# A check at the seam of two stages: most of it is emitted into the attention, and its end is cut to one maximum

## The chip, the cores and the metric

The kernel runs on one core of one Trainium2 chip. Five engines work side by side, each with its own stream of instructions in program order: PE (TensorE, matrix products), DVE (VectorE), ACT (ScalarE), POOL (GpSimd) and SP (SyncE, which here issues most DMAs). The metric is the device time of one execution in microseconds, median of several runs.

## The reference

An attention in which each query keeps only its 32 largest scores feeds a mixture of experts with a greedy, capacity-bound assignment of tokens.

```python
scores = scale * np.matmul(q, k.transpose(0, 1, 3, 2))       # batch 8, heads 8, seq 576, head_dim 64
kth = np.partition(scores, -32, axis=-1)[..., -32:-31]
scores = np.where(scores >= kth, scores, -1000000000.0)
attn = np.exp(scores - np.max(scores, axis=-1, keepdims=True))
attn = attn / (np.sum(attn, axis=-1, keepdims=True) + 1e-09)
x = heads_side_by_side(np.matmul(attn, v))                   # 4608 tokens x 512
logits = x @ w_gate                                          # 8 experts
order = np.argsort(-logits.flatten())
for idx in order:                                            # each token to one expert, 576 per expert
    tok, e = (int(idx) // E, int(idx) % E)
    if assigned[tok] >= 0 or counts[e] >= cap: continue
    assigned[tok] = e; counts[e] += 1
for e in range(E):
    mask = assigned == e
    out[mask] = np.maximum(x[mask] @ w1[e], 0.0) @ w2[e]
```

## The kernel before

The kernel has three parts, one after the other: `attention`, `redo` and `moe`.

`attention` works on 32 pairs of heads (8 batches, 4 pairs each). A pair has 9 tiles of 128 queries against 576 keys. For each tile PE makes the scores (L218) in one of three PSUM buffers; DVE finds maxima of six chunks (L221, called `c0` to `c5` in the plan) and ranks them (L224 to L228, `k0` to `k4`) to the 24th largest; ACT takes a sign against it and counts into one column of `acc` (L233); DVE writes a filling (L239), PE shifts the kept scores away and back (L236), DVE finds the next eight maxima, of which the 32nd largest is one (L240); ACT makes the mask (L243). Later, in `soft`, PE computes transposed scores with the mask (L281 to L287), ACT the exponential (L291), POOL splits it into two halves of float16 by a copy and a subtraction (L294, L297), and PE multiplies with V (L365). `tail` does the same for the last 64 keys (L319 to L327). DVE and ACT normalise (L345 to L347). POOL copies each pair's thresholds into `cuts` (L309). After the third pair of a batch, and again after the fourth, `logits` adds its part of x @ w_gate to the tile `L` (last additions L421 and L422), and `store` writes x to DRAM.

The order in which the instructions are emitted comes from a list planner on the host (`Plan`): every step has an engine, an assumed duration, predecessors and a due time; on each engine, among the steps that can start within a small window, the one with the smallest due time is emitted next. A due time is the tile's nominal start (4.9146 per tile) plus an offset from the table `O`, for instance 138.764 for `c0`, 131.547 for `c2` and 127.672 for `c5`. The chip's engines then run their streams in that order.

After the planned part, `verdict` (L424 and following) tests whether the fast way of finding thresholds was right everywhere: for all 288 tiles the count in `acc` must be a whole number in bounds and the threshold positive, and every logit must be finite. It sums the good ones per pair and per group of logits over partitions by a product with ones on PE (L447), and writes one flag per pair and the number of flags set (L448 to L454). Then `redo` loads that number into a register of every engine (L485) and branches (L486); in its body, which isn't entered for these inputs, flagged pairs are computed again in a slow and exact way.

`moe` then picks the experts in turn from `L` by bisection, gathers the tokens, and runs the two matrix products. Its first steps on DVE are at L621 and following.

Of the kernel before, what the change touches and what calls it, by code (L numbers as in the profile page):

```python
# [7 lines left out]
F32 = mybir.dt.float32  # L8
# [88 lines left out]

VS=64.0
QS=256.0
def attention(tc, q,k,v,w_gate,x_out,L,flags, pairs):  # L100
    NCH=6
    nc=tc.nc
    CW=576//NCH; NCAND=8*NCH
    with ExitStack() as ctx:
# [284 lines left out]
        def logits(P,part):  # L389
# [28 lines left out]
            else:  # L418
# [2 lines left out]
                piece(0,[lambda c=c: P["x"][0][:,c,384:512] for c in range(4)],512,dots,lambda lg: V.tensor_tensor(main.rearrange("p c e -> p (c e)"),lg[:,:32],main.rearrange("p c e -> p (c e)"),op=ALU.add))  # L421
                piece(1,*corner(1),lambda lg: V.tensor_tensor(last,lg[o:o+64,:8],last,op=ALU.add))  # L422
            P["fin"]=at(t0,lambda: None,fin); P["lgdone"]=fin[-1]
        def verdict():  # L424

            n9=len(pairs)*9; npr=len(pairs)
            c=cp.tile([128,n9],F32,name="vc"); r=cp.tile([128,n9],F32,name="vr"); ok=cp.tile([128,n9],F32,name="vok")
            V.tensor_scalar(c,acc,-0.5,-256.0,op0=ALU.mult,op1=ALU.add)
            V.tensor_scalar(r,c,12582912.0,None,op0=ALU.add)
            V.tensor_scalar(r,r,-12582912.0,None,op0=ALU.add)  # L430
            V.tensor_tensor(ok,r,c,op=ALU.is_equal)
            V.scalar_tensor_tensor(ok,c,8.0,ok,op0=ALU.is_le,op1=ALU.mult)
            V.scalar_tensor_tensor(ok,c,0.0,ok,op0=ALU.is_ge,op1=ALU.mult)
            V.scalar_tensor_tensor(ok,cuts,0.0,ok,op0=ALU.is_gt,op1=ALU.mult)
            good=cp.tile([128,npr+4],F32,name="good")
            V.tensor_reduce(good[:,:npr],ok.rearrange("p (n i) -> p n i",i=9),axis=AX.X,op=ALU.add)
            whole=[]
            for k,(u0,u1) in enumerate(((0,28),(32,35),(28,32),(35,36))):
                Lf=L[:,u0:u1,:].rearrange("p t e -> p (t e)"); w=8*(u1-u0); fin=cp.tile([128,w],F32,name=f"fin{k}")
                V.tensor_tensor(fin,Lf,Lf,op=ALU.subtract)  # L440
                V.tensor_scalar(fin,fin,0.0,None,op0=ALU.is_equal)
                V.tensor_reduce(good[:,npr+k:npr+k+1],fin,axis=AX.X,op=ALU.add); whole.append(128.0*w)
            ones=cp.tile([128,1],F32,name="ones1"); V.memset(ones,1.0)
            want=cp.tile([1,npr+4],F32,name="want"); V.memset(want[:,:npr],1152.0)
            for k,x_ in enumerate(whole): V.memset(want[:,npr+k:npr+k+1],x_)
            pt=ps_t.tile([128,512],F32,tag="pt",name="ptv")
            T.matmul(pt[:1,:npr+4],ones,good,start=True,stop=True)  # L447
            bad=cp.tile([1,npr+4],F32,name="bad"); V.tensor_tensor(bad,want,pt[:1,:npr+4],op=ALU.subtract)  # L448
            nf=cp.tile([1,1],F32,name="nf"); V.tensor_reduce(nf,bad[:,npr:],axis=AX.X,op=ALU.add)
            V.tensor_scalar(bad[:,:npr],bad[:,:npr],nf,None,op0=ALU.add)  # L450
            fl=cp.tile([1,npr],F32,name="flf"); V.tensor_scalar(fl,bad[:,:npr],0.0,None,op0=ALU.not_equal)
            V.tensor_reduce(nf,fl,axis=AX.X,op=ALU.add)
            V.tensor_copy(flags[:,npr:npr+1],nf)
            V.tensor_copy(flags[:,0:npr],fl)  # L454

        Ps={}; batch={}
        for n in range(len(pairs)):
            prep(n); P=Ps[n]; b=P["b"]
            P.update(st=None,tr={},mx={},rel={},q2={},ev={},teh={},soft={},x=[None,None])
            first=P["hp"]==0  # L460
            def begin(P=P,n=n,first=first):
                P["st"]=wk.tile([128,9,33],F32,tag="st",name="st",bufs=3)
                P["x"]=(wk.tile([128,4,512],F32,tag="xb",name="xb",bufs=2),wk.tile([128,4,64],F32,tag="xr",name="xr",bufs=2)) if first else Ps[n-1]["x"]
            pre=[Ps[n-3]["done"]] if n>2 else []
            if n: pre.append(Ps[n-1]["begin"])
            if first and b>1: pre.append(batch[b-2])
            P["begin"]=at(n*9*PER+O["S"]-0.01,begin,pre)
            for i in range(9): tile_ops(P,i)
            for i in range(9): soft(P,i)
            clear(P)  # L470
            tail(P)
            values(P)
            if P["hp"]==2: logits(P,0)
            if P["hp"]==3:
                P["done"]=at(P["done"]["t"]+.001,lambda: None,[P["done"],Ps[n-1]["fin"]])
                logits(P,1); P["done"]=P["fin"]; batch[b]=at((n*9+8)*PER+O["lg"]+O["lgd"]*5,lambda P=P: store(P),[P["fin"]],e="D",d=2.0,late=4.0)
        loom.run()
        verdict()


def redo(tc,q,k,v,w_gate,x,L,flags):

    nc=tc.nc
    V,G,A,T=nc.vector,nc.gpsimd,nc.scalar,nc.tensor
    any_=nc.values_load(flags[0:1,32:33],min_val=0,max_val=32)  # L485
    with tc.If(any_>0):  # L486
        with ExitStack() as ctx:
            cp=ctx.enter_context(tc.tile_pool(name="rc",bufs=1))
            wk=ctx.enter_context(tc.tile_pool(name="rw",bufs=2))
            ps=ctx.enter_context(tc.tile_pool(name="rps",bufs=2,space=PSUM))  # L490
            ident=cp.tile([128,128],F32,name="identr"); make_identity(nc,ident)
            wg=cp.tile([128,4,8],F32,name="wgf"); nc.sync.dma_start(out=wg,in_=w_gate.rearrange("(c p) e -> p c e",p=128))
            qv,kv,vv=(t.rearrange("b (g t) s d -> b g t s d",t=2) for t in (q,k,v))
# [102 lines left out]
def moe(tc, K, L, x, w1, w2, out):  # L596
# [4 lines left out]
    with ExitStack() as ctx:  # L601
# [3 lines left out]
        wp=ctx.enter_context(tc.tile_pool(name="wp",bufs=2))  # L605
        ps=ctx.enter_context(tc.tile_pool(name="ps",bufs=1,space=PSUM))
        V,G,A,P,S=nc.vector,nc.gpsimd,nc.scalar,nc.tensor,nc.sync
        O=dict(RT=341.23, TE=-289.219, TN=-172.671, WT=261.813, XT=32.643, RD=-297.654, GL=2.6, W_V=0.1, W_A=0.395, W_G=2.142, W_P=0.0, W_D=9.225, WD0=678.788, WD1=322.634, RA=-247.153, WT0=9.992, TE0=-55.559, XT0=-502.675)
        GL,RT,TE,TN,WT,XT,RD,RA,WT0,TE0,XT0=(O[k] for k in ('GL','RT','TE','TN','WT','XT','RD','RA','WT0','TE0','XT0')); WD=(O['WD0'],O['WD1'])
        WIN={e:O['W_'+e] for e in 'VAGPD'}  # L610
        HOW0='vvvvvvvv'; HOW='vvvvvvvv'; GP=3; AHV=1; JO=1; PB=3; SPN=512
        plan=Plan(dict(ph=4,po=2,wr=4,W=2,xT=2,hh=1,xg=4,ob=3),WIN);
# [319 lines left out]
        c=Chain(-RT)  # L932
        for p in range(E):
            c.pre=[X[p-1]["next"]]+([X[p-2]["idx"]] if p>1 else []) if p else []
            c.t=p*47.0-RT
            route(p,c)
            enlist(p,Chain(c.t+(TE if p else TE0),X[p]["sel"],X[p-1]["idx"] if p else None))
            weigh(p,p*47.0-(WT if p else WT0))
            bring(p,p*47.0-XT if p else XT0)
            ffn(p,p*47.0)  # L940
# [3 lines left out]
def attention_then_moe(tc, q, k, v, w_gate, w1, w2, out):  # L944
    with ExitStack() as ctx:
        dp = ctx.enter_context(tc.tile_pool(name="dp", bufs=1, space=DRAM))
        lp = ctx.enter_context(tc.tile_pool(name="lp", bufs=1))
        x = dp.tile([4608, 512], F32, name="x")
        L = lp.tile([128, 36, 8], F32, name="L")
        pairs = [(b, hp) for b in range(8) for hp in range(4)]  # L950
        flags = lp.tile([1, 40], I32, name="flags")
        K = moe_consts(tc, lp)
        attention(tc, q, k, v, w_gate, x, L, flags, pairs)
        redo(tc, q, k, v, w_gate, x, L, flags)
        moe(tc, K, L, x, w1, w2, out)


# [25 lines left out]
```

## Time and profile before

| | us |
|---|---|
| median of 3 runs | 1455.42 (1453.14 to 1456.38) |
| the profiled execution | 1456.97 |
| its span, from the first instruction to the last | 1455.2 |
| DVE busy in the span | 1208.0 (83%) |
| PE busy | 1291.6 (89%) |
| POOL busy | 878.1 (60%) |
| ACT busy | 863.5 (59%) |

The profiled execution is 1.55 us above the median of the others. Times within the trace count from the span's start. A share of busy time is a mean over stages which have different limits, so it says little by itself about one place.

### The profile page before, as it was taken

What the parts mean: (1) busy time and instruction counts of PE and PEld (TensorE: products, weight loads), DVE (VectorE), ACT (ScalarE), POOL (GpSimd) and SP (SyncE); (2) the same over time, 40 slices, a digit from 0 to 9 for tenths busy, and PEclk for the clock granted to TensorE, in tenths of its full rate; (3) what the DMA queues carried; (4) which work ended last, traced back from release to release, by engine and by line L of the source; (5) the groups of instructions that cost most, each with busy time, mean ns of one, the idle gap of its engine ahead of it and who ended that gap; (6) DMA issues with size and microseconds to landing.
All of it is one profiled execution on the core that took longest, in us unless ns stands there. A gap on an engine that the chain in (4) does not pass through costs nothing. (4 is left out here: it accounts for less than half of the span.)

```text
span 1455.2 us, 41655 instructions
## 1 busy us (share of the span) xinstructions
PE 1291.6 (89%) x15019; PEld 908.3 (62%) x15020; DVE 1208.0 (83%) x6010; ACT 863.5 (59%) x1898; POOL 878.1 (60%) x1285
## 2 busy tenths in 40 slices
PE   2889999999999999999999999834989999999997
PEld 1667776776776766776676776723655655655663
DVE  5899999899999999999999999578879878878510
ACT  2677777777777777787787787603324424424421
POOL 5687888798798788789789879402123123133211
PEclk8899999999999999999999999955999999999999
DMA  5434444444345444454445442104336447448500
GB/s 123 90 84 75 113 100 86 102 87 99 94 95 106 78 111 91 85 117 90 88 113 85 87 110 43 41 6 148 132 83 200 145 83 199 145 87 279 114 33 33
DMA packets 293384, 148.47 MB, mean 102 GB/s; under 512 B 250672, under 2 KB 275248, under 8 KB 292144
## 3 DMA queue, kind: packets, MB, share of 16 engines
q1 hardware_dynamic: 287280, 126.84, 38.4%
q0 software_dynamic: 5888, 18.88, 4.4%
q8 instruction: 120, 1.97, 0.6%
q14 instruction: 96, 0.79, 0.2%
HBM read 71.34 MB, written 18.87 MB: 62 GB/s over the span
## 5 line engine op out<-in xcount | busy, mean ns | idle before, releaser
L221 DVE MAX8 cd<-s 128x8 f32<-128x96 f32 x1728 | 373.5, 252 | 35.3 <-PE s L218 30.6
L297 POOL TENSOR_TENSOR elm<-F,ehm 128x512 f16<-128x512 f32 x256 | 294.7, 1157 | 7.9
L243 ACT ACTIVATE r<-s,st 128x576 bf16<-128x576 f32 x288 | 213.2, 740 | 106.5 <-PE s L236 70.5
L233 ACT ACTIVATE w<-s,st 128x576 uint16<-128x576 f32 x288 | 213.5, 741 | 79.7 <-DVE st L229 76.8
L240 DVE MAX8 st<-s 128x8 f32<-128x584 f32 x288 | 220.8, 767 | 7.4 <-PE s L236 2.6
L218 PE MATMUL s<-K,Q 128*128 128x512 f16 (+3 forms) x1280 | 193.0, 291 | 27.8 <-DMA Q<-nq 20.2
L890 PE MATMUL ph<-xT,w1h 128*128 128x288 f16 x1024 | 196.3, 289 | 2.7 <-DMA xT<-xs 2.2
L929 POOL DMA_INDIRECT out_dram<-ob,idx x40 | 54.9, 1372 | 223.8 <-ACT ob L924 157.4
L287 PE MATMUL pt<-Q,K 66*128 66x128 f16 (+1 forms) x1280 | 179.1, 216 | 0.1
L286 PE MATMUL pt<-Q,K 128*128 128x128 f16 (+1 forms) x1280 | 178.2, 215 | 0.0
L294 POOL TENSOR_SCALAR ehm<-F 128x512 f16<-128x512 f32 x256 | 157.2, 620 | 32.3 <-ACT F L291 29.8
L218 PEld LDWEIGHTS <-Q 128*128 128x128 f16 (+1 forms) x1280 | 104.8, 103 | 108.5 <-DMA Q<-nq 19.9
L236 PE MATMUL s<-w,off 128*128 128x512 f16 x576 | 132.6, 288 | 38.6 <-DVE s L239 30.3
L850 POOL DMA_INDIRECT xg<-x,idx x40 | 51.7, 1292 | 179.0 <-DVE idx L796 107.3
L291 ACT ACTIVATE F<-pt 128x512 f32<-128x512 f32 x256 | 150.7, 597 | 14.8 <-PE pt L287 9.9
L890 PE MATMUL ph<-xT,w1l 128*128 128x288 f16 x512 | 148.1, 289 | 0.0
L365 PE MATMUL pv<-vt,E 128*64 128x65 f32 (+1 forms) x1024 | 146.8, 257 | 0.3 <-DVE L L416 0.3
L236 PE MATMUL s<-w,back 128*128 128x512 f16 x576 | 118.7, 288 | 20.6 <-DVE st L240 18.3
L899 ACT ACTIVATE hh<-ph 128x288 f16<-128x288 f32 x128 | 52.4, 410 | 130.1 <-PE ph L890 125.6
L286 PEld LDWEIGHTS <-K 128*128 128x128 f16 x1280 | 117.2, 99 | 18.4 <-issue 5.5
L365 PEld LDWEIGHTS <-ehm 128*128 128x128 f16 x2048 | 115.9, 101 | 9.8
L365 PEld LDWEIGHTS pv<-vt,E 128*64 128x64 f32 (+1 forms) x1024 | 113.2, 164 | 13.5 <-issue 3.1
(262 smaller groups left out, 3342.4 us busy)
## 6 DMA issues: line engine op xcount, KB each, us to landing
wr<-in_moe_w_dram SPq DMA_DIRECT2D x32, 1024.0 KB, 9.5
kn<-in_k_dram SPq DMA_DIRECT2D x64, 128.0 KB, 2.4
qn<-in_q_dram SPq DMA_DIRECT2D x64, 128.0 KB, 2.3
vn<-in_v_dram SPq DMA_DIRECT2D x64, 128.0 KB, 2.3
x<-xb SPq DMA_DIRECT2D x8, 1024.0 KB, 4.6
Q<-nq SPq DMA_TRANSPOSE x160, 2.5
kn<-in_k_dram SPq DMA_DIRECT2D x64, 16.0 KB, 2.2
qn<-in_q_dram SPq DMA_DIRECT2D x64, 16.0 KB, 2.1
```

Of the source, the lines that this page charges most:

```text
L218: T.matmul(s_ps[rows,a:b_],P[Q][:,qc],P[K][:,h*576+a:h*576+b_],start=(Q=="Q1"),stop=(Q=="Q2"))
L221: V.max(D["cd"][:,c*8:c*8+8],D["s"][:,576*c//NCH:576*(c+1)//NCH])
L233: A.activation(D["w"],D["s"][:,:576],AF.Sign,bias=P["st"][:,i,32:33],scale=(1+2.0**-21),accum_out=acc[:,col])
L236: T.matmul(D["s"][:,a:b_],by,w[:,a:b_],start=False,stop=True,skip_group_check=True)
L240: def next8(): V.max(P["st"][:,i,24:32],D["s"][:,:584])
L243: A.activation(r,D["s"][:,:576],AF.Relu,bias=P["st"][:,i,31:32],scale=-1.0)
L286: T.matmul(o,K2[:,kb:kb+128],Q1[:,qc],start=False,stop=False,skip_group_check=True)
L287: T.matmul(o,K3[0:66,kb:kb+128],Q2[0:66,qc],start=False,stop=(c==3 and h==sub[-1][0]),skip_group_check=True)
L294: G.tensor_scalar(D["eh"],D["E"],1.0,0.0,op0=ALU.mult,op1=ALU.add)
L297: G.tensor_tensor(el,D["E"],D["eh"],op=ALU.subtract); P["e"][i]=(D["eh"],el)
L365: for m_ in (range(N-1) if part==0 else (N-1,)): T.matmul(out,seq[m_][0],seq[m_][1],start=(m_==0),stop=(m_==N-1))
L890: P.matmul(B["ph"][:,:288],a[:,c,fs],xT[:,b+c,cs],start=(i==0),stop=(i==11))
```

## The change

The check is taken apart. `judge(n0,n1)` holds its eight steps for the thresholds of some pairs, `finite(k)` its three steps for one group of logits; each returns its steps as a list of functions. `ahead` hands the thresholds of the first 30 pairs and the logits of the first seven batches (two groups) to the planner, as DVE steps of an assumed 0.35 us that follow one another, with the last tile's nominal start as their due time and with the cuts of pairs 28 and 29, or the end of pair 27, as predecessors. `verdict` does the rest, the last two pairs and the last batch's two groups, with the three chains interleaved. After the sum on PE it takes one maximum over what is missing, and writes the minimum of it and 1 as the flag that is branched on. The sums over the flags, and the flags of the single pairs, are made inside the branch of `redo`, from the tile `bad`, which is now allocated outside. The constants `ones` and `want` are set before the planned part. A name `R1` with the value 0.0 is added to a due time in `moe`.

```diff
-def attention(tc, q,k,v,w_gate,x_out,L,flags, pairs):
+def attention(tc, q,k,v,w_gate,x_out,L,flags,bad, pairs):
...
+        npr=len(pairs); spans=((0,28),(32,35),(28,32),(35,36)); early=npr-2
+        good=cp.tile([128,npr+4],F32,name="good"); ones=cp.tile([128,1],F32,name="ones1"); V.memset(ones,1.0)
+        want=cp.tile([1,npr+4],F32,name="want"); V.memset(want[:,:npr],1152.0)
+        for s_,(u0,u1) in enumerate(spans): V.memset(want[:,npr+s_:npr+s_+1],128.0*8*(u1-u0))
+        def judge(n0,n1):
+            cs=slice(n0*9,n1*9); w=9*(n1-n0); B={}
+            def a0(): B["c"]=cp.tile([128,w],F32,name=f"vc{n0}"); V.tensor_scalar(B["c"],acc[:,cs],-0.5,-256.0,op0=ALU.mult,op1=ALU.add)
+            def a1(): B["r"]=cp.tile([128,w],F32,name=f"vr{n0}"); V.tensor_scalar(B["r"],B["c"],12582912.0,None,op0=ALU.add)
+            def a2(): V.tensor_scalar(B["r"],B["r"],-12582912.0,None,op0=ALU.add)
+            def a3(): B["ok"]=cp.tile([128,w],F32,name=f"vok{n0}"); V.tensor_tensor(B["ok"],B["r"],B["c"],op=ALU.is_equal)
+            def a4(): V.scalar_tensor_tensor(B["ok"],B["c"],8.0,B["ok"],op0=ALU.is_le,op1=ALU.mult)
+            def a5(): V.scalar_tensor_tensor(B["ok"],B["c"],0.0,B["ok"],op0=ALU.is_ge,op1=ALU.mult)
+            def a6(): V.scalar_tensor_tensor(B["ok"],cuts[:,cs],0.0,B["ok"],op0=ALU.is_gt,op1=ALU.mult)
+            def a7(): V.tensor_reduce(good[:,n0:n1],B["ok"].rearrange("p (n i) -> p n i",i=9),axis=AX.X,op=ALU.add)
+            return [a0,a1,a2,a3,a4,a5,a6,a7]
+        def finite(k):
+            u0,u1=spans[k]; w=8*(u1-u0); Lf=L[:,u0:u1,:].rearrange("p t e -> p (t e)"); B={}
+            def a0(): B["f"]=cp.tile([128,w],F32,name=f"fin{k}"); V.tensor_tensor(B["f"],Lf,Lf,op=ALU.subtract)
+            def a1(): V.tensor_scalar(B["f"],B["f"],0.0,None,op0=ALU.is_equal)
+            def a2(): V.tensor_reduce(good[:,npr+k:npr+k+1],B["f"],axis=AX.X,op=ALU.add)
+            return [a0,a1,a2]
+        def ahead():
+            t=((npr-1)*9+8)*PER
+            for fs,pre in ((judge(0,early),[Ps[early-1]["clear"],Ps[early-2]["clear"]]),(finite(0),[Ps[npr-5]["done"]]),(finite(1),[Ps[npr-5]["done"]])):
+                for f in fs: pre=[at(t,f,pre,e="V",d=.35)]
         def verdict():
...
+            j_,f2,f3=judge(early,npr),finite(2),finite(3)
+            for a in (f2[0],f3[0],j_[0],f2[1],f3[1],j_[1],f2[2],f3[2],*j_[2:]): a()
             pt=ps_t.tile([128,512],F32,tag="pt",name="ptv")
             T.matmul(pt[:1,:npr+4],ones,good,start=True,stop=True)
-            bad=cp.tile([1,npr+4],F32,name="bad"); V.tensor_tensor(bad,want,pt[:1,:npr+4],op=ALU.subtract)
-            nf=cp.tile([1,1],F32,name="nf"); V.tensor_reduce(nf,bad[:,npr:],axis=AX.X,op=ALU.add)
-            V.tensor_scalar(bad[:,:npr],bad[:,:npr],nf,None,op0=ALU.add)
-            fl=cp.tile([1,npr],F32,name="flf"); V.tensor_scalar(fl,bad[:,:npr],0.0,None,op0=ALU.not_equal)
-            V.tensor_reduce(nf,fl,axis=AX.X,op=ALU.add)
-            V.tensor_copy(flags[:,npr:npr+1],nf)
-            V.tensor_copy(flags[:,0:npr],fl)
+            V.tensor_tensor(bad,want,pt[:1,:npr+4],op=ALU.subtract)
+            m=cp.tile([1,1],F32,name="most"); V.tensor_reduce(m,bad,axis=AX.X,op=ALU.max)
+            V.tensor_scalar(flags[:,npr:npr+1],m,1.0,None,op0=ALU.min)
...
+        ahead()
         loom.run()
         verdict()
...
-    any_=nc.values_load(flags[0:1,32:33],min_val=0,max_val=32)
+    any_=nc.values_load(flags[0:1,32:33],min_val=0,max_val=1)
     with tc.If(any_>0):
...
+            nf=cp.tile([1,1],F32,name="nf"); V.tensor_reduce(nf,bad[:,32:],axis=AX.X,op=ALU.add)
+            V.tensor_scalar(bad[:,:32],bad[:,:32],nf,None,op0=ALU.add)
+            fl=cp.tile([1,32],F32,name="flf"); V.tensor_scalar(fl,bad[:,:32],0.0,None,op0=ALU.not_equal)
+            V.tensor_copy(flags[:,0:32],fl)
...
-            c.t=p*47.0-RT
+            c.t=p*47.0-RT+(R1 if p==1 else 0)
```

## Rows read from the trace of the kernel before

**Rows 1.** Stretches: us, each engine's busy time (instructions), PE's clock, DMA share, GB/s.

```profile
877.00:909.00 32.00, 29.72 (x414) 21.47 (x414) 30.05 (x172) 24.88 (x59) 29.88 (x47) 1.00 0.25 48
...
947.00:955.00 8.00, 0.28 (x2) 0.12 (x2) 6.46 (x33) 0.00 (x0) 0.00 (x0) 0.50 0.00 0
```

**Rows 2.** Timeline of DVE, last logits to first step of moe: start, length, line.

```profile
946.58 0.17 DVE L422 TENSOR_TENSOR L<-lg,L 64x8 f32<-64x8 f32 x1 [0.34 <-PE lg L410]
946.76 0.31 DVE L428 TENSOR_SCALAR vc<-acc 128x288 f32<-128x288 f32 x1
...
947.79 0.46 DVE L431 TENSOR_TENSOR vok<-vr,vc 128x288 f32<-128x288 f32 x1
...
950.20 0.38 DVE L440 TENSOR_TENSOR fin<-L 128x224 f32<-128x224 f32 x1
...
952.48 0.17 DVE L441 TENSOR_SCALAR fin<-fin 128x8 f32<-128x8 f32 x1
952.69 0.16 DVE L442 TENSOR_REDUCE good<-fin 128x1 f32<-128x8 f32 x1
...
953.32 0.18 DVE L448 TENSOR_TENSOR bad<-want,ptv 1x36 f32<-1x36 f32 x1 [0.39 <-PE ptv L447]
...
954.46 0.16 DVE L454 CAST flags<-flf 1x32 int32<-1x32 f32 x1
960.12 0.07 DVE L621 MEMSET pen<- 128x8 f32 x1 [5.50 <-SPq L486]
```

**Rows 3.** DVE's waits from 845 to 928: total us, times, longest us.

```profile
DVE cd L221 <- PE s L218: 0.8, 3, 0.3
...
DVE st L240 <- PE s L236: 0.2, 1, 0.2
```

**Rows 4.** Timeline of DVE in moe, two chains interleaved, eight starts apart.

```profile
986.97 0.23 DVE L756 TENSOR_SCALAR w8c<-rev,win 128x8 f32<-128x8 f32 x1
...
987.84 0.45 DVE L667 TENSOR_TENSOR ml<-L,pen 128x288 f32<-128x288 f32 x1
988.21 0.19 DVE L771 SCALAR_TENSOR_TENSOR qf<-qf 128x36 f32<-128x36 f32 x1
```

**Rows 5.** Timelines of POOL and DVE, what the moved steps must follow.

```profile
876.25 0.21 POOL L309 TENSOR_SCALAR cuts<-st 128x9 f32<-128x9 f32 x1
...
848.69 0.14 DVE L422 TENSOR_TENSOR L<-lg,L 64x8 f32<-64x8 f32 x1
```

**Rows 6.** Timelines of POOL and DVE at the kernel's start.

```profile
2.80 0.65 POOL L592 IOTA exf<- 32x512 f32 x1
...
2.79 0.18 DVE L576 CAST tk<-thi 128x36 f32<-128x36 int32 x1
2.88 0.61 DVE L576 CAST tk<-tlo 128x36 f32<-128x36 int32 x1
```

**Rows 7.** POOL's two lines of soft: shortest, median, longest in ns; first and last start.

```profile
L294 POOL TENSOR_SCALAR ehm<-F x256: 614/620/627, 38.4 to 936.6; 128x512 f16<-128x512 f32 x128
...
L297 POOL TENSOR_TENSOR elm<-F,ehm x256: 1149/1157/1168, 39.1 to 937.3; 128x512 f16<-128x512 f32 x128
```

**Rows 8.** Timelines of DVE, POOL, ACT and PE in the attention's drain.

```profile
929.73 0.77 DVE L240 MAX8 st<-s 128x8 f32<-128x584 f32 x1 [0.56 <-PE s L236]
...
933.75 0.60 ACT L327 ACTIVATE E<-pt 128x512 f32<-128x512 f32 x1 [0.25 <-PE pt L324]
...
935.45 0.19 PE L365 MATMUL pv<-vh,ehm 128*128 128x65 f16 x1
...
938.12 0.16 DVE L345 TENSOR_SCALAR rs<-pv 128x4 f32<-128x4 f32 x1 [6.92 <-PE pv L365]
...
916.00 0.20 POOL L265 TENSOR_SCALAR m<-st 128x3 f32<-128x3 f32 x1 [5.45 <-DVE st L224]
...
937.26 1.15 POOL L297 TENSOR_TENSOR elm<-F,ehm 128x512 f16<-128x512 f32 x1
```

**Rows 9.** Timeline of DVE, its first step of the planned part.

```profile
21.43 1.42 DVE L221 MAX8 cd<-s 128x8 f32<-128x96 f32 x8 [13.73 <-PE s L218]
```

More of the change, by code (lines that the diff above doesn't have):

```diff
@@ L423, in logits @@
             P["fin"]=at(t0,lambda: None,fin); P["lgdone"]=fin[-1]
-        def verdict():
[L426 to L445, printed above, removed]
@@ L476, in attention, with redo @@
                 logits(P,1); P["done"]=P["fin"]; batch[b]=at((n*9+8)*PER+O["lg"]+O["lgd"]*5,lambda P=P: store(P),[P["fin"]],e="D",d=2.0,late=4.0)
+        ahead()
         loom.run()
         verdict()
-def redo(tc,q,k,v,w_gate,x,L,flags):
+def redo(tc,q,k,v,w_gate,x,L,flags,bad):
     nc=tc.nc
     V,G,A,T=nc.vector,nc.gpsimd,nc.scalar,nc.tensor
-    any_=nc.values_load(flags[0:1,32:33],min_val=0,max_val=32)
+    any_=nc.values_load(flags[0:1,32:33],min_val=0,max_val=1)
     with tc.If(any_>0):
@@ L607, in moe @@
         V,G,A,P,S=nc.vector,nc.gpsimd,nc.scalar,nc.tensor,nc.sync
-        O=dict(RT=341.23, TE=-289.219, TN=-172.671, WT=261.813, XT=32.643, RD=-297.654, GL=2.6, W_V=0.1, W_A=0.395, W_G=2.142, W_P=0.0, W_D=9.225, WD0=678.788, WD1=322.634, RA=-247.153, WT0=9.992, TE0=-55.559, XT0=-502.675)
-        GL,RT,TE,TN,WT,XT,RD,RA,WT0,TE0,XT0=(O[k] for k in ('GL','RT','TE','TN','WT','XT','RD','RA','WT0','TE0','XT0')); WD=(O['WD0'],O['WD1'])
+        O=dict(RT=341.23, R1=0.0, TE=-289.219, TN=-172.671, WT=261.813, XT=32.643, RD=-297.654, GL=2.6, W_V=0.1, W_A=0.395, W_G=2.142, W_P=0.0, W_D=9.225, WD0=678.788, WD1=322.634, RA=-247.153, WT0=9.992, TE0=-55.559, XT0=-502.675)
+        R1,GL,RT,TE,TN,WT,XT,RD,RA,WT0,TE0,XT0=(O[k] for k in ('R1','GL','RT','TE','TN','WT','XT','RD','RA','WT0','TE0','XT0')); WD=(O['WD0'],O['WD1'])
         WIN={e:O['W_'+e] for e in 'VAGPD'}
@@ L951, in attention_then_moe @@
         flags = lp.tile([1, 40], I32, name="flags")
+        bad = lp.tile([1, 36], F32, name="bad")
         K = moe_consts(tc, lp)
-        attention(tc, q, k, v, w_gate, x, L, flags, pairs)
-        redo(tc, q, k, v, w_gate, x, L, flags)
+        attention(tc, q, k, v, w_gate, x, L, flags, bad, pairs)
+        redo(tc, q, k, v, w_gate, x, L, flags, bad)
         moe(tc, K, L, x, w1, w2, out)
```

## Prediction

> **What bounds the kernel now.** I read the table of stretches first. Up to 930 us the attention keeps PE, DVE and POOL busy together: of 32 us between 877 and 909, DVE works 30.05 and POOL 29.88. Between 947 and 955 only DVE works, POOL and DMA not at all, and PE sits at a granted clock of 0.50 [rows 1]. That hole is the step that the change cuts. The timeline of DVE shows what is in it: the last logits are added at 946.58 (done 946.75), then verdict() runs as one chain until the flags are written at 954.46 + 0.16 = 954.62, and DVE does nothing more until 960.12 [rows 2]. So the check costs 7.87 us with no cover, and 5.50 us follow in which all engines read the flag and jump over redo(). There is no work of verdict() in those, so I leave them as they are.
>
> Next I ask what bounds the place to which the work goes. The list of DVE's waits between 845 and 928 holds four entries, one of 0.8 us and three of 0.2 us, 1.4 us in 83 [rows 3]. DVE waits for nobody there: in that part it is the bound, or so near to it that whatever is added to its stream comes out later at its end.
>
> **What verdict() still costs.** 17 DVE instructions stay between the last logits and the flag: six for the logits of the last batch, eight on 18 columns for the last two pairs, then subtraction, maximum and minimum with the write. The trace has prices for both kinds of spacing. Small instructions that need not wait for each other start 0.11 us apart (eight starts from 986.97 to 987.84, 0.87 us) [rows 4]. One that needs its predecessor starts 0.21 us after it (952.48 to 952.69) [rows 2]. The first nine are interleaved three ways, so they take the short spacing: first start 946.76, ninth at 946.76 + 8 x 0.11 = 947.64. Five more each need the one before: 947.64 + 5 x 0.21 = 948.69, done 0.18 later at 948.87. The sum over partitions on PE: from the last reduction's end (952.69 + 0.16 = 952.85) to the subtraction's start at 953.32 are 0.47 us [rows 2], of which about 0.08 were memsets that now run at the kernel's start: 0.39, so 949.26. Maximum and minimum each 0.21 later: 949.68, done 949.82. The flag is there 954.62 - 949.82 = **4.8 us** earlier. If nothing overlaps, 13 x 0.21 replaces 8 x 0.11 + 5 x 0.21 and 4.0 are left; if the first starts ahead of the last logits, 4.9. The flags of the single pairs move into the branch, which isn't entered, and cost nothing.
>
> **What moves into the attention.** Fourteen DVE instructions: eight on 270 columns for the first 30 pairs, three on 224 and three on 24 for the early logits. Their due time in the plan is that of the last tile, (31 x 9 + 8) x 4.9146 = 1410.5. The plan takes, among what DVE can start at once, what has the smallest due time. A tile's first chunk maximum has its tile's start + 138.8, the third + 131.5, the sixth + 127.7, so from tile 259 on (in pair 28) these come after 1410.5, and the moved steps go ahead of them as soon as they are ready. Ready means: after pair 29's cuts, on POOL at 876.25, and after the logits of pair 27, whose last addition is at 848.69 [rows 5]. I therefore expect them near 849 and from 877 to 887, not in the drain. They bring no DMA.
>
> Their time on DVE: a 288-wide one-source step takes 0.31, a two-input step 0.46 [rows 2], and with an independent neighbour the next one starts 0.08 before the end (0.45 long, next start after 0.37) [rows 4]. Eight steps: 3 x 0.23 + 4 x 0.38 + 0.37 = 2.58, for 270 columns 2.4. The three on 224 columns, of which the first took 0.38 [rows 2], about 0.8, the three on 24 at 0.1 each 0.3: 3.5 us. Some fall between two steps of a rank chain that would start 0.21 apart and then fill a gap of 0.1 each, at most 1.4 for fourteen; I take half: **2.8 us** (2.1 if all do so, 4.6 if nothing overlaps).
>
> Then POOL. At the kernel's start a one-source DVE step of 36 columns begun at 2.79 takes 0.18 us. Its twin, begun at 2.88 beside POOL's iota of 2.80 to 3.45, takes 0.61 and ends at 3.49, just after POOL [rows 6]. So a one-source step between SBUF tiles is held until POOL's running instruction ends. In the attention before the change none is held and none holds: POOL's 256 copies and 256 subtractions lie within 614 to 627 and 1149 to 1168 ns [rows 7], since DVE there reads scores from PSUM or runs at the single rate. Five of the fourteen are one-source steps that run at the double rate (0.31 against 0.46 for the same 288 columns). POOL is busy 0.93 of the time [rows 1], with instructions of 0.62 and 1.16 us by turns; what is left of the running one when DVE arrives is on the mean (0.62² + 1.16²) / (2 x 1.78) = 0.485 us, times 0.93 = 0.45. Five cost **2.25 us**. Six others read two SBUF tensors each; no row shows such a step beside POOL. Bounds are nothing and the same 0.45 each, 2.7; I take the middle, **1.35**, since the held rows are like them in having both ends in SBUF and unlike in rate. The three reductions I count as free. What is queued behind a held step is the running tile's rank chain and fill, for which ACT's sign (L233) and PE's move (L236) wait.
>
> The Trainium skill (SBUF — State Buffer, section "Who interferes with whom") speaks against the change here: it says that a DVE instruction with two SBUF inputs also contends with a GpSimd instruction that reads SBUF, and that the second to come blocks wholly. By it all eleven would be held, 4.95 us in place of my 3.6; the rows of the start agree with it for one-source steps (0.61 against 0.18 us), and no run here yet shows the other kind.
>
> DVE falls behind by 2.8 + 2.25 + 1.35 = 6.4 us. What takes some back: half of its 1.4 us of waits (0.7), and slack in the drain. Its last maximum is at 929.73; the exponential of the tail ends at 933.75 + 0.60 = 934.35, and the products with V, which need it, begin at 935.45 [rows 8]: 1.1 us of slack, of which I count half, as the order there is laid down beforehand. 6.4 - 1.2 = **5.2 us later** at the end of the attention.
>
> The six memsets at the start stand ahead of 13.73 us in which DVE waits for the first scores [rows 9]: free; without that cover some 0.4 us. The name R1 is 0.0 and changes no due time. After the flag the same work follows in the same order, so everything shifts as one.
>
> Sum: -4.8 + 5.2 = +0.4 us. The profiled execution took 1456.97 (span 1455.2), 1.55 above the median of 1455.42; it would come out at 1457.4, the median at **1455.8**. A difference of 0.2%, 2.9 us, is about what can be told from no change.
>
> **Rivals.**
> First, nothing is held. The trace's even POOL times speak for it only in that DVE hasn't tried; the start's rows speak against. Then 2.8 - 1.2 = 1.6 is paid: 1455.4 - 4.8 + 1.6 = 1452.2, faster.
> Second, the moved steps end up in the drain after all, in the 6.92 us in which DVE waits before 938.12 [rows 8]. POOL is still at work there, but nothing hangs on DVE: 1450.6. Against it stand the due times above.
> Third, the six two-input steps are held like the five: 11 x 0.45 = 4.95 in place of 3.6, + 1.35, so 1457.2, still no difference that can be told. It is what the rule of the Trainium skill quoted above (SBUF — State Buffer) would give.
> Fourth, slower: the held steps also hold POOL, and POOL's queue decides the drain. POOL works in order; at 916.00 it stands 5.45 us for a maximum of DVE's, and its last instruction ends at 937.26 + 1.15 = 938.41 [rows 8], just ahead of the last products. If DVE's lateness keeps that queue standing until one more copy and subtraction (1.78 us) lands behind the last maximum, nothing is absorbed either: 6.4 + 1.78 = 8.2, 1455.4 - 4.8 + 8.2 = 1458.8. It costs time from an end of the attention 4.8 us later, and tells from 7.7. Those 5.45 us, which are slack of POOL's, speak against.
>
> **How the numbers follow.** My forecast 0.40, nothing held 0.20, in the drain 0.10, all held 0.15, POOL's queue 0.15. Faster 0.30 (first and second), same 0.55 (forecast and third), slower 0.15 (fourth). The forecast's own range, with its bounds, is 1453.0 to 1458.0. The asked range leaves out the second rival and the upper half of the fourth: 1451.3 to 1458.8.
>
> **What would show it.** After: flags about 3.1 us behind the last logits; the 270-wide steps near 877 to 890, some of the one-source ones of 0.5 to 1.2 us in place of 0.3, and POOL instructions above 627 and 1168 ns; the last logits near 952 in place of 946.75; from there to the end the old distance. Wrong would be: steps in the drain, no stretched step beside a busy POOL, or a DVE that starts to wait for PE behind them.

## The result, and the profile after

The changed kernel takes 1463.22 us (median of 19 runs, 1457.48 to 1471.0) against 1456.15 for the kernel before (19 runs, 1452.34 to 1459.57): ratio 1.0060, 95% interval 1.0046 to 1.0074. That is 8.7 us slower (6.7 to 10.8), where 0.4 was forecast and the range ended at 1458.8. (The ratio is the one on record, not the quotient of the two medians; that gives 7.1 us, within the interval.) The profiled execution is the longest of the 19: 1471.0, span 1469.3.

The stretches, with the columns of [rows 1]: us, busy time and number of instructions of PE, PEld, DVE, ACT, POOL, then PE's granted clock, DMA share, GB/s.

```profile
877.00:909.00 32.00, 26.84 (x341) 19.73 (x341) 28.77 (x145) 20.84 (x48) 25.89 (x36) 0.95 0.24 45
909.00:930.00 21.00, 17.78 (x219) 12.69 (x219) 17.21 (x100) 12.20 (x27) 9.12 (x19) 0.84 0.06 11
947.00:958.00 11.00, 10.16 (x140) 9.81 (x140) 0.51 (x3) 2.51 (x8) 5.54 (x7) 0.69 0.01 1
964.00:968.00 4.00, 0.28 (x2) 0.11 (x2) 2.17 (x17) 0.00 (x0) 0.00 (x0) 0.50 0.00 0
```

The hole in which DVE works alone has shrunk by more than half [rows 1], as meant. But between 877 and 909 every engine now does less: PE 26.84 in place of 29.72, POOL 25.89 in place of 29.88, DVE 28.77 in place of 30.05. And the granted clock of PE, 1.00 before from 877 to 930, is 0.95 and then 0.84 there, and 0.69 in the drain, the attention's end behind the last maximum (0.50 is the 1.2 GHz level, 1.00 the 2.4 GHz one). DVE has the early steps on top of its work in this stretch and is busy for less of it, so it waits. The lateness isn't the time of its added steps alone.

The timeline of DVE around the flag, of the changed kernel:

```profile
963.75 0.17 DVE L422 TENSOR_TENSOR L<-lg,L 64x8 f32<-64x8 f32 x1 [0.33 <-PE lg L410]
963.95 0.27 DVE L443 TENSOR_TENSOR fin<-L 128x32 f32<-128x32 f32 x2
...
965.74 0.17 DVE L438 TENSOR_REDUCE good<-vok 128x2 f32<-128x18 f32 x1
966.37 0.18 DVE L458 TENSOR_TENSOR bad<-want,ptv 1x36 f32<-1x36 f32 x1 [0.46 <-PE ptv L457]
...
966.80 0.14 DVE L460 TENSOR_SCALAR flags<-most 1x1 int32<-1x1 f32 x1
```

From the end of the last logits (963.92) to the flag (966.94) are 3.02 us, against 7.87 in [rows 2]: 4.85 saved, as forecast. But the last logits come at 963.75, 17.2 us later than before.

The early steps in the same kernel's timeline of DVE, and the first step behind them that waits:

```profile
881.46 0.31 DVE L431 TENSOR_SCALAR vc<-acc 128x270 f32<-128x270 f32 x1
...
881.81 0.59 DVE L432 TENSOR_SCALAR vr<-vc 128x270 f32<-128x270 f32 x1
...
883.06 1.27 DVE L434 TENSOR_TENSOR vok<-vr,vc 128x270 f32<-128x270 f32 x1
...
885.68 1.26 DVE L436 SCALAR_TENSOR_TENSOR vok<-vc,vok 128x270 f32<-128x270 f32 x1
...
892.05 0.16 DVE L345 TENSOR_SCALAR rs<-pv 128x4 f32<-128x4 f32 x1 [1.74 <-PE pv L365]
```

Beside them, in the timeline of POOL:

```profile
882.84 1.19 POOL L297 TENSOR_TENSOR elm<-F,ehm 128x512 f16<-128x512 f32 x1
...
885.31 1.33 POOL L297 TENSOR_TENSOR elm<-F,ehm 128x512 f16<-128x512 f32 x1
```

The steps stand where they were expected. L434 and L436, two-input steps that take 0.46 on 288 columns alone [rows 2], take 1.27 and 1.26 and end at 884.33 and 886.94, just behind POOL's subtractions (884.03 and 886.64). POOL is held too: 1.33 where the longest subtraction before was 1.168 [rows 7]. The last line of DVE is new in kind: it waits 1.74 us for a product with V. [rows 3] show no wait for that product, and the waits for PE there are 0.3 at most. Now they are:

```profile
DVE cd L221 <- PE s L218: 1.9, 3, 1.2
DVE st L240 <- PE s L236: 1.8, 2, 1.6
DVE rs L345 <- PE pv L365: 1.7, 1, 1.7
```

(DVE's waits of the changed kernel, 845 to 928: total us, times, longest.) That was the sign named beforehand for a wrong forecast: "a DVE that starts to wait for PE behind them".

One thing the diff doesn't show is plain once the streams of the two programs are laid side by side. Apart from the check's own steps, the order of all other instructions in the two traces is the same up to about 850 us, and then different, up to the end of the attention: in 66 of 1205 places on POOL, 109 of 1626 on ACT, 319 of 4875 on DVE and 768 of 11536 on PE. (The expectations below count places on another base.) So two things changed, work and order, and four programs take them apart: the changed kernel, drain, order_only and work_only.

### The profile page after: what moved, and what is told of

Same layout as the page of the kernel before. It is cut to its first block, busy times and chain, and to the rows that moved or that the text cites. A ratio compares the mean times of both kernels' runs of the same rounds, so it can differ in the third digit from the quotient of the medians.

```text
span 1469.3 us, 41662 instructions
## 1 busy us (share of the span) xinstructions
PE 1299.5 (88%) x15019; PEld 913.9 (62%) x15020; DVE 1210.7 (82%) x6014; ACT 862.8 (59%) x1898; POOL 876.3 (60%) x1285
## 5 line engine op out<-in xcount | busy, mean ns | idle before, releaser
L240 DVE MAX8 st<-s 128x8 f32<-128x584 f32 x288 | 220.7, 766 | 9.6 <-PE s L236 4.7
L287 PE MATMUL pt<-Q,K 66*128 66x128 f16 (+1 forms) x1280 | 180.0, 216 | 1.1 <-DMA Q<-nq 1.1
L291 ACT ACTIVATE F<-pt 128x512 f32<-128x512 f32 x256 | 150.7, 596 | 19.8 <-PE pt L287 13.1
L365 PE MATMUL pv<-vt,E 128*128 128x65 f32 (+1 forms) x1024 | 148.5, 259 | 0.3 <-DVE L L416 0.3
L365 PEld LDWEIGHTS <-ehm 128*128 128x128 f16 x2048 | 119.0, 103 | 9.6
L365 PEld LDWEIGHTS pv<-vt,E 128*128 128x128 f32 (+1 forms) x1024 | 114.7, 166 | 14.0 <-issue 3.4
```

The source lines that it names most:

```text
L240: def next8(): V.max(P["st"][:,i,24:32],D["s"][:,:584])
L287: T.matmul(o,K3[0:66,kb:kb+128],Q2[0:66,qc],start=False,stop=(c==3 and h==sub[-1][0]),skip_group_check=True)
L365: for m_ in (range(N-1) if part==0 else (N-1,)): T.matmul(out,seq[m_][0],seq[m_][1],start=(m_==0),stop=(m_==N-1))
```

## Experiments

**How the runs are read.** The time from the load of the flag to the end of the kernel is 494.4 to 502.3 us in the fourteen profiles, with no relation to what was changed. Totals of few runs therefore tell a few us only as intervals. Within the attention the starts of L240 (one per tile, 288 in all) are the better clock. "Lag" below is the start of the last L240 minus that of the kernel before (929.73 [rows 8]), less the same difference at the 251st (814.26 before), which takes out what each execution had won or lost by then (2.7 us or less). "To logits" is from the last L240 to the last logits L422 (before: 946.58 - 929.73 = 16.85). Each was read from that run's timeline of DVE. The last column is the measured ratio less 1, times the median of before, in us; the difference of the two medians lies up to 1.7 us from it, within the interval each time. So differences of a us or two between runs are read from the lag and the way to the logits. These come from one profiled execution of each program, two of the changed kernel.

| run | order of the other instructions | early steps | lag, us | to logits, us | against before, us (95%) |
|---|---|---|---|---|---|
| drain | as before | in the drain | -0.31 | 16.45 | -5.8 (-8.4 to -3.1) |
| work_only | as before | in place | 7.49 | 16.44 | +2.9 (+0.4 to +5.4) |
| order_only | as changed | in the drain | 7.67 | 22.45 | +8.0 (+5.2 to +10.6) |
| changed kernel | as changed | in place | 11.55 | 21.85 | +8.7 (+6.7 to +10.8) |
| again | as changed | in place | 11.65 | 18.68 | one run |
| spread0 | as before | one per tile | 5.36 | 16.40 | +2.2 (-0.1 to +4.4) |
| half | as before | in place, 135 columns | 6.63 | 16.40 | +0.4 (-2.0 to +2.9) |
| d10 | entries of 0.10 | in the drain | 0.94 | 16.40 | -5.4 (-7.9 to -2.9) |
| tiny | entries of 0.02 | in the drain | 2.02 | 18.40 | -2.6 (-4.8 to -0.6) |
| fin_order | six entries of 0.35 | in the drain | 4.28 | 17.64 | -0.4 (-3.1 to +2.2) |
| true57 | planned with 0.57 | in place | 7.88 | 20.24 | +4.8 (+2.9 to +6.8) |
| all_drain | as before | all 32 pairs in the drain | -0.32 | 16.42 | -4.9 (-7.1 to -2.9) |

**drain: the order of before, the steps in the drain.**

```diff
-            t=((npr-1)*9+8)*PER
-            for fs,pre in ((judge(0,early),[Ps[early-1]["clear"],Ps[early-2]["clear"]]),(finite(0),[Ps[npr-5]["done"]]),(finite(1),[Ps[npr-5]["done"]])):
-                for f in fs: pre=[at(t,f,pre,e="V",d=.35)]
+            t=((npr-1)*9+8)*PER; end=list(Ps[npr-1]["rel"].values())
+            for fs in (judge(0,early),finite(0),finite(1)):
+                pre=end
+                for f in fs: pre=[at(t,f,pre,e="V",d=.35)]
```

> The fourteen early steps are planned behind the relus of the last pair, so they stand after the last maximum L240; the order of all other instructions on every engine is that of the kernel before. Both theories: the early steps are hidden in DVE's wait of 6.92 us of [rows 8], the flag stays 4.8 us earlier, 1451.3 (1450 to 1453), that is -4.8. If the change has another cost outside the attention's end (the memsets, the branch, the start), it is still there and the time stays above 1455.

1449.25 (12 runs), 5.8 us faster than before. The gain is the flag's 4.8 us, and the fourteen steps are hidden in the wait of [rows 8]. Nothing else in the change costs anything that this run could see. Its last L240 and its last logits:

```profile
929.18 0.77 DVE L240 MAX8 st<-s 128x8 f32<-128x584 f32 x1 [0.55 <-PE s L236]
...
945.63 0.17 DVE L422 TENSOR_TENSOR L<-lg,L 64x8 f32<-64x8 f32 x1 [0.19 <-PE lg L410]
```

**order_only: the order of the changed kernel, the steps in the drain.**

```diff
+            for n_,pre in ((8,[Ps[early-1]["clear"],Ps[early-2]["clear"]]),(3,[Ps[npr-5]["done"]]),(3,[Ps[npr-5]["done"]])):
+                for f in range(n_): pre=[at(t,lambda: None,pre,e="V",d=.35)]
             for fs in (judge(0,early),finite(0),finite(1)):
                 pre=end
```

> The plan of the changed kernel with fourteen empty entries of 0.35 us where its early steps stood, so that all other instructions have the changed kernel's order; the early steps themselves run in the drain as in the run beside it. Theory ORDER (the entries make the plan order the last three pairs worse, and that costs what the result shows beyond the steps' own time): 1458 or more. Theory WORK (the steps' time on DVE, with what waits for it, costs it all): 1451.3, within 1.5 us of the run with the steps in the drain.

1462.55, 8.0 us slower than before and 13.8 than the run with the steps in the drain, for entries that emit nothing. ORDER is right: fourteen empty entries cost as much as the whole change. The same two lines here:

```profile
936.55 0.78 DVE L240 MAX8 st<-s 128x8 f32<-128x584 f32 x1 [0.50 <-PE s L236]
...
959.00 0.17 DVE L422 TENSOR_TENSOR L<-lg,L 64x8 f32<-64x8 f32 x1 [0.34 <-PE lg L410]
```

**work_only: the order of before, the steps in place.**

```diff
-                for f in fs: pre=[at(t,f,pre,e="V",d=.35)]
+                for f in fs: pre=[at(t,f,pre,e="V",d=0.0)]
```

> The early steps at the places of the changed kernel, but entered in the plan with a duration of 0, so that all other instructions have the order of the kernel before. Theory WORK: 1463 as the changed kernel. Theory ORDER: only the steps' own lateness of some 5 us is left against the gain of 4.8, 1455 to 1457.

1456.52, 2.9 us slower (0.4 to 5.4). That is ORDER's number, not WORK's 1463. The last L240 is late, and the way from it to the logits is the same as in drain:

```profile
937.39 0.78 DVE L240 MAX8 st<-s 128x8 f32<-128x584 f32 x1 [0.55 <-PE s L236]
...
953.83 0.17 DVE L422 TENSOR_TENSOR L<-lg,L 64x8 f32<-64x8 f32 x1 [0.18 <-PE lg L410]
```

The stretch from 848 us to the last L240, first of drain, then of work_only, then of order_only:

```profile
848.00:929.30 81.30, 75.93 (x1058) 57.35 (x1058) 75.53 (x434) 64.13 (x149) 63.83 (x102) 1.00 0.29 61
```

```profile
848.00:937.40 89.40, 78.33 (x1060) 58.48 (x1058) 82.26 (x451) 64.66 (x149) 65.09 (x101) 0.98 0.28 56
```

```profile
848.00:936.60 88.60, 79.30 (x1030) 58.72 (x1028) 75.50 (x427) 62.21 (x146) 61.50 (x97) 0.94 0.29 54
```

The two losses are of about one size and of different kinds. With the work, DVE is busy 6.7 us longer (82.26 against 75.53) and idle 1.4 us longer (7.1 against 5.8). With the order, DVE's busy time is the same (75.50) and its idle time goes from 5.8 (81.30 - 75.53) to 88.60 - 75.50 = 13.1 us: it waits. PE then has the granted clock at 0.94, and POOL has started 97 instructions by the last L240 in place of 102: it has more left for the drain.

One place shows how an order makes DVE wait. The timelines of PE and DVE in order_only:

```profile
907.10 0.21 PE L236 MATMUL s<-w,off 128*128 128x64 f16 x1 [0.74 <-DVE s L239]
...
908.54 0.27 PE L287 MATMUL pt<-Q,K 66*128 66x128 f16 x1 [0.69 <-DMA Q<-nq]
...
909.24 0.68 PE L236 MATMUL s<-w,back 128*128 128x512 f16 x2
909.73 0.67 PE L236 MATMUL s<-w,off 128*128 128x512 f16 x2
```

```profile
910.44 0.77 DVE L240 MAX8 st<-s 128x8 f32<-128x584 f32 x1 [1.35 <-PE s L236]
```

and in drain, for the same L240 (the 280th):

```profile
904.56 0.39 PE L236 MATMUL s<-w,off 128*128 128x512 f16 x1
904.78 0.39 PE L281 MATMUL pt<-nid,r 128*128 128x128 bf16 x4
...
905.26 0.19 PE L236 MATMUL s<-w,off 128*128 128x64 f16 x1
```

```profile
905.52 0.76 DVE L240 MAX8 st<-s 128x8 f32<-128x584 f32 x1
```

In both orders a softmax product (L281 to L287) stands in PE's stream ahead of a move that DVE needs. In the changed order it takes columns of Q that a DMA is still transposing: PE waits 0.69 us for them in its turn, the moves stand behind it and take from 909.24 to 910.40, and DVE waits 1.35. In the order of before the product there waits for nobody, and DVE comes to its L240 without a wait. The stretches there, order_only and then drain, show what else happened:

```profile
902.00:906.00 4.00, 2.22 (x16) 1.04 (x14) 3.74 (x24) 2.78 (x6) 3.67 (x8) 1.00 0.02 5
906.00:910.00 4.00, 2.57 (x17) 1.71 (x17) 3.02 (x20) 1.27 (x3) 0.47 (x1) 0.58 0.12 24
910.00:914.00 4.00, 4.00 (x32) 2.42 (x31) 2.33 (x11) 2.85 (x6) 3.35 (x5) 0.57 0.00 0
```

```profile
902.00:906.00 4.00, 3.90 (x58) 2.79 (x56) 3.92 (x27) 3.72 (x8) 3.92 (x6) 1.00 0.00 0
906.00:910.00 4.00, 3.80 (x70) 3.05 (x67) 3.59 (x20) 2.94 (x8) 3.63 (x7) 1.00 0.12 25
910.00:914.00 4.00, 4.00 (x79) 3.35 (x75) 3.79 (x25) 2.29 (x7) 0.00 (x0) 1.00 0.02 4
```

PE stood idle 1.8 of the four us to 906, then its granted clock went to 0.58 and 0.57, and it was busy all of 910 to 914 with 32 matmuls, where drain, with another mix of them, has 79. Two such moves take 0.68 us here and 0.41 at a clock of 1.00.

**spread0: the order of before, one early step per tile.** Each step is bound behind the relu of another tile, `pre+[rel(g+j)]`, with a duration of 0.

> As the run with the steps at their places and the order of before, but each of the eight 270-wide steps bound behind the relu of another tile of pair 30, each of the six for the logits behind one of pair 29: one step per tile, not eight in a row. Theory BURST (eight steps in 5 us hold up the rank chains so long that PE runs dry and its granted clock falls to 0.50, which costs more than the steps): the granted clock stays at 1.00 up to the last maximum, 1455 to 1457. Theory SUM (each microsecond on DVE costs one wherever it stands): as the run with the steps at their places, within 1.5 us.

The granted clock stays at 1.00 to the last L240 (in work_only it is 0.95 and 0.89 between 877 and 900), and the lag is 5.36 in place of 7.49. That is BURST's sign, and spreading the steps saves 2.1 us of lag; how much of that is the clock and how much the rank chains that are held up less long isn't measured apart. The totals (+2.2 and +2.9) can't tell BURST from SUM.

**half: the eight steps on 135 columns.** `judge(0,15)` stands in place and `judge(15,30)` in the drain.

> As the run with the steps at their places and the order of before (7.5 us late at the last maximum, of which 5.7 at the eight steps), but the eight steps cover 135 columns (15 pairs) there, and the other 135 are judged in the drain. Theory HOLD (a step waits out POOL's running instruction, whatever its width): the steps still take up to 1.2 us, some 1.2 us of the 5.7 are saved, 1 to 2 us faster than with 270 columns. Theory WIDTH (the steps' own time counts): half of the 5.7, 2.9 us, is saved.

The lag falls by 0.86 to 6.63: HOLD (1.2) and not WIDTH (2.9). The totals (+0.4 and +2.9) can't decide it. One step shows it, in the timeline of DVE here (135 columns) and in work_only (270), with POOL's subtractions beside the first:

```profile
883.63 1.14 DVE L436 SCALAR_TENSOR_TENSOR vok<-vc,vok 128x135 f32<-128x135 f32 x1
```

```profile
885.46 1.28 DVE L436 SCALAR_TENSOR_TENSOR vok<-vc,vok 128x270 f32<-128x270 f32 x1
```

```profile
882.28 2.33 POOL L297 TENSOR_TENSOR elm<-F,ehm 128x512 f16<-128x512 f32 x2
```

Half the columns, nearly the same time: it ends at 884.77, 0.16 behind POOL's pair of subtractions (884.61). What a step pays is what is left of POOL's running instruction when it arrives, and that can be nothing. In work_only the two-input step L434 takes no longer than alone:

```profile
883.52 0.44 DVE L434 TENSOR_TENSOR vok<-vr,vc 128x270 f32<-128x270 f32 x1
```

**tiny, d10, fin_order: what in the entries makes the order worse.** They are order_only with `d=.02`, with `d=.10`, and without the eight entries of `judge`.

> As the run with the empty entries, but each entry is planned with 0.02 us in place of 0.35, 0.28 us in all; the steps themselves in the drain. The order of all other instructions still departs from that of before, from the same place on (first on POOL at its 1079th of 1185, in over a thousand places on PE). Theory LATENESS (the order is worse because the plan believes DVE 4.9 us later and lets PE, POOL and ACT drift to another pace): with 0.28 us nothing is lost, within 2 us of the run with the steps in the drain, 3 to 6 us faster than before. Theory LOTTERY (the plan takes what is due first among what can start, so any entry turns some choices over, and an order that was measured and kept is traded for one that wasn't): slower than the run in the drain by 4 to 13 us, that is from 1 us faster than before to 8 us slower.

> The run with the empty entries, each planned with 0.10 us in place of 0.35, 1.4 in all; steps in the drain. Theory LATENESS (the loss grows with the time that the plan believes taken from DVE): between the entries of 0.02 (2.6 us faster than before) and those of 0.35 (8.0 slower), 1 us faster to 3 slower than before. Theory LOTTERY (it goes by which choices turn over): PE's order departs from that of before in 552 places, half as many as with 0.02 (1122), so the loss against the steps in the drain is no larger than there, 3 to 6 us faster than before.

> Only the six empty entries of the logits' checks, 0.35 us each, near 849; those of the eight steps are gone, and all steps stand in the drain. PE's order departs in 1053 places. Theory LATENESS: 2.1 of 4.9 us, so 6 of the 13.8 us of loss: 0 to 2 us slower than before. Theory BURST (the eight entries in a row near 881 make the order worse): 4 to 6 us faster than before, as the run with the steps in the drain. Theory LOTTERY: neither sum need hold; the time can lie anywhere from 5 us faster to 8 slower.

By their totals, entries of 0.28 us in all lose 3.2 us against drain (-2.6 against -5.8), those of 1.4 us lose 0.4, the six of 2.1 us lose 5.4, all fourteen of 4.9 us lose 13.8. By lag and way to the logits together it is 4.3, 1.2, 5.8 and 14.0. So tiny was too dear for LATENESS and, by its total, a little cheap for LOTTERY; d10 then came out below tiny with five times the planned time and half the changed places, which LATENESS excludes and LOTTERY said; fin_order sits between. The loss isn't a function of the planned time. That leaves which steps happen to change places; it is what is left over, and wasn't shown step by step. By lag and way to the logits the order of before was better than the four others, by little in d10 (1.2 us, which the totals can't tell). Why each is worse was followed at one place only (above).

**true57: the steps in place, planned with what they take.**

```diff
-                for f in fs: pre=[at(t,f,pre,e="V",d=.35)]
+                for f in fs: pre=[at(t,f,pre,e="V",d=.57)]
```

> The changed kernel with its early steps in place and planned with 0.57 us each in place of 0.35, near to what they took (7.5 us of lateness for 14 steps). Theory PLAN-TRUE (the loss comes from a plan that believes the wrong duration): the order fits the lateness, and only the work is paid, at most 3 us slower than before. Theory LOTTERY: an order like that of the changed kernel, 6 to 13 us slower than before.

4.8 us slower (2.9 to 6.8): neither theory's number, between them. A truer duration gives a better order than 0.35 did (+8.7), but no better than leaving the order alone (+2.9; by lag and way to the logits together 28.1 us against 23.9). So a wrong duration isn't the whole cause, and one more order can't show whether it is a part of it.

**fill: keeping PE busy by hand.** 16 matmuls on constants stand in front of PE's moves and scores of four tiles of order_only.

```diff
+            def idle(k):
+                for _ in range(k): T.matmul(LS[-1][:,592:1008],nid60,dum,start=True,stop=True,skip_group_check=True)
```

> The run with the empty entries (order of the changed kernel, steps in the drain), with 16 idle matmuls of 416 bf16 columns on constants put in front of PE's moves and scores of tiles 277 to 280, into unused columns of the scores' tile, where PE stood idle 2.5 us in five pieces before its granted clock went to 0.58. Nothing of the result is left out. Theory CLOCK (part of the order's loss is PE at 1.2 GHz): the granted clock stays at 1.00 over those 12 us, DVE's two waits of 1.35 and 1.17 there go below 1 us in sum, and the last maximum is 1.5 to 3 us less late than the 7.7 of the run without; 1459.5 to 1461. Theory ORDER ALONE (the clock costs nothing, DVE waits because the instructions stand in the wrong place): 7.7 or, with PE's extra 2.7 us, up to 9.

1465.44, 10.2 us slower than before (6.3 to 14.1). The fillers write beside the last 64 score columns of the scores' tile, and the kernel's result changes by them, against the expectation; the run is read for the clock and the waits alone. The granted clock did stay at 1.00 there, but the lag is 7.40 against 7.67: four of the groups of fillers stood waiting for DVE's chunk maxima, 0.43 + 1.22 + 0.63 + 0.78 = 3.1 us, and what stood behind them waited too. It tells nothing between CLOCK and ORDER ALONE. Besides, the clock is 0.50 from 866 to 869 in order_only, ahead of the first filler, and 1.00 in fill, so more than the fillers differs.

**again: the changed kernel a second time.**

> The changed kernel once more, unaltered, for a second profile. Theory FIXED (the attention's loss is the same in every execution, and what scatters by up to 13 us lies behind the flag, 494 to 502 us in the profiles so far): the last maximum is 11.5 us late, within 1, and the last logits stand 21.9 us behind it. Theory CHANCE (the profiled execution was the longest of 19, because its attention ran badly): 8 us late or less at the last maximum, or a drain shorter than 20 us.

1467.03. The lag is 11.65 against 11.55, so FIXED up to the last L240. But the way to the logits is 18.68 in place of 21.85, so CHANCE behind it, and the same time (502.3) follows the flag in both. The program is the same, so the two executions tell, for the drain, what fill couldn't: what the clock costs. The stretches in the drain, of the changed kernel and then of again (0.83 us earlier at the last L240):

```profile
949.00:951.00 2.00, 1.44 (x21) 1.27 (x22) 0.00 (x0) 0.99 (x3) 1.92 (x4) 0.61 0.00 0
951.00:953.00 2.00, 2.00 (x29) 2.00 (x28) 0.00 (x0) 0.00 (x0) 1.71 (x2) 0.50 0.00 0
953.00:955.00 2.00, 2.00 (x27) 2.00 (x25) 0.16 (x1) 0.00 (x0) 0.00 (x0) 0.50 0.00 0
```

```profile
949.00:951.00 2.00, 2.00 (x46) 1.99 (x47) 0.00 (x0) 0.28 (x1) 1.92 (x3) 1.00 0.00 0
951.00:953.00 2.00, 2.00 (x50) 2.00 (x49) 0.34 (x2) 0.78 (x4) 0.95 (x1) 1.00 0.00 0
953.00:955.00 2.00, 1.81 (x33) 1.72 (x29) 0.49 (x3) 0.45 (x3) 0.00 (x0) 1.00 0.03 8
```

and the first sums of the last values on DVE, likewise:

```profile
954.81 0.16 DVE L345 TENSOR_SCALAR rs<-pv 128x4 f32<-128x4 f32 x1 [6.74 <-PE pv L365]
```

```profile
951.75 0.16 DVE L345 TENSOR_SCALAR rs<-pv 128x4 f32<-128x4 f32 x1 [4.51 <-PE pv L365]
```

With the granted clock at 0.50 PE does 27 to 29 matmuls in 2 us, at 1.00 it does 46 to 50. The fall costs 21.85 - 18.68 = 3.2 us of the drain in one execution and nothing in the other. In order_only (22.45) it fell too. What PE did just before doesn't tell the two executions apart: it was busy 3.90 of the 4.45 us before the fall, and 3.87 of 4.40 in again, with the same wait at the end, the changed kernel first:

```profile
949.74 0.47 PE L398 MATMUL ptl<-identf,xr 128*128 128x128 f32 x1 [0.56 <-ACT F L291]
```

```profile
948.91 0.33 PE L398 MATMUL ptl<-identf,xr 128*128 128x128 f32 x1 [0.56 <-ACT F L291]
```

Why the clock fell in one of them alone isn't shown, and whether both ran on the same chip isn't on record. The Trainium skill (TensorE: Matmul & The Clock Gate, section "HAM oscillation — how this bites in real kernels") has it that a wait of PE that is long enough lets its clock fall to half, so that the work behind it starts slow. The trace of order_only agrees in that 0.58 followed PE's idle time at 902 to 906, above, but that idle time came in pieces of 0.83 us at most; and again shows a wait without a fall.

**all_drain: the whole of the thresholds in the drain.** `judge(0,npr)` at the places of drain, its seventh step behind the last cuts, and only the six steps for the last logits in `verdict`.

> The candidate for the best version: as the run with the steps in the drain, but all 32 pairs are judged there (its last test bound behind the last cuts on POOL), so that behind the last logits only the two checks of the logits, the sum over partitions and the flag are left. Five chained steps and three interleaved ones less: 5 x 0.21 + 3 x 0.11 = 1.4 us earlier than the run in the drain if the drain hides the wider steps, so about 7 us faster than before; if DVE is late for the sums of the last values, no faster than that run.

1449.13, 4.9 us faster than before (2.9 to 7.1), which can't be told from drain. In its profile the flag's load follows the start of the last logits after 1.96 us, against 3.23 in drain, as it should; 1.3 us are less than the rest of the kernel scatters. It beats both kernels, as do drain, d10 and, by less, tiny.

## Why the prediction was wrong

- **The flag, -4.8: right.** 7.87 became 3.02, and drain measures -5.8 (-8.4 to -3.1) for it.
- **DVE as the bound, and the places of the steps: right.** They stand at 850.5 to 854.0 and 881.5 to 888.6 against "near 849 and from 877 to 887".
- **Occupancy and holds, 6.4: the size nearly right, by errors that partly cancel.** With the order kept the lag is 7.49. In work_only each held step's length, less what its like takes alone, gives 2.2 us for the six two-input steps, put at 1.35, and 0.9 for the five one-source steps, put at 2.25: 3.0 held in place of 3.6. Of the 6.7 us that DVE is busy longer, that leaves some 3.7 for occupancy, put at 2.8. (The split is an estimate from that timeline.) The rule of the Trainium skill that was weighed there (SBUF — State Buffer, section "Who interferes with whom") was right that two-input steps are held: L436 takes 1.28 beside POOL. But that the sum with its 4.95 comes to 7.75, near 7.49, is luck, since 4.95 takes the same mean hold for every step, and what was left of POOL's instruction ran from nothing (L434, 0.44) to 0.85.
- **Absorbed, -1.2: wrong.** The way from the last L240 to the logits is 16.44 with the lateness and 16.45 without, so the drain took back nothing. And DVE's waits up to there didn't shrink by 0.7 but grew by 1.4. With 7.5 for the lateness and nothing absorbed the sum is -4.8 + 7.5 = +2.7; work_only measures +2.9.
- **The step that failed: the sum had no term for the order of everything else.** The prediction used the planner to find where the steps would go, then let all other instructions keep their places and be late with DVE ("DVE falls behind by 6.4 us"). But an entry in the plan moves the plan's DVE time, and from there each choice behind it. That alone costs 13.8 us when the steps stand elsewhere, and 5.8 on top of the steps (+8.7 against +2.9). The two don't add: lags of 7.5 and 7.7 make 11.6. That DVE waits partly while it would have been late anyway would explain it, but no run was made for that.
- **The rivals.** The third (all held) had the right mechanism for the work, with too small an end. The fourth, slower through POOL's queue, had the direction and a part of the mechanism, with the wrong cause. In the changed kernel 12 POOL instructions start behind the last L240 in place of 10, the one more copy and subtraction that it named, and POOL's last one ends 10.9 us behind the last L240 in place of 8.7 (11.6 in order_only). In again, without a fall of the clock, the way to the logits is longer by about as much. But lateness alone doesn't bring it about: in work_only POOL ends 8.7 behind. The first (nothing held) is refuted by the steps of 1.26 and 1.27 us. The second (in the drain) was the kernel that should have been written: -4.8 forecast, -5.8 measured (-8.4 to -3.1).
- **What stays open.** How much of the order's 7.7 us up to the last L240 is the granted clock and how much the waits that brought it down; fill didn't separate them. Nor is it shown why the clock falls in one execution of a program and not in another.

## What to carry to other kernels

In a kernel whose order comes from a list planner, a new entry is two changes, the work and a new order of all that follows. Lay the streams side by side before counting microseconds, and let the work in with a duration of zero, or behind the last thing that the order turns on, if the order is to be kept. And put such work where an engine waits anyway, not where it could first run: here the same fourteen steps cost 8 to 9 us in the full stretch and nothing 50 us later.

## What the runs showed of the hardware

- Two executions of one program, alike to 0.1 us from the 251st to the last L240, part by 3.2 us behind it, where PE's granted clock fell to 0.50 in one and not in the other, after the same busy time and the same waits. Whether this is behind the changed kernel's spread (13.5 us over 19 runs against 7.2) is open: only two of its executions were profiled, and the kernel before spreads by 14.25 us over the 29 runs measured beside drain.
- A two-input DVE step between SBUF tiles that meets a running POOL subtraction ends just behind it: 0.3 us behind with 270 columns, 0.16 with 135, 0.04 with 24. So its width hardly counts (1.28 us for 270 columns, 1.14 for 135), and a step of 24 columns took 1.09 us where its like alone takes 0.17. POOL's subtractions went up to 1.33 us in the changed kernel, from 1.168 at most.
